# Attention scores from split one-pass products, with filler products in the routing and two conversions moved

## The chip, the cores and the metric

The kernel runs on one core of one Trainium2 chip. The metric is the time of one execution in device microseconds; of the kernel before, three runs gave 955.38, 954.65 and 955.22 us, a median of 955.22.

## The reference

Three blocks follow each other. All inputs are float32.

```python
# attention with a sigmoid: q, k, v are (4, 12, 448, 64)
scores = q @ k.T / sqrt(64) - log(448)
attn   = sigmoid(scores)
x      = (attn @ v), heads put together       # (1792, 768)

# routing: every token gets one of 8 experts, 224 tokens each at most,
# the pairs (token, expert) taken greedily in the order of the logits
logits = x @ w_gate                           # (1792, 8)
out[tokens of e] = relu(x[tokens of e] @ w1[e]) @ w2[e]     # 768 -> 1024 -> 768

# a dense block: 768 -> 2048 -> 768
g = s * relu(x @ w_in) ** 2 + b
y = g @ w_out
```

The weights of the dense block arrive as 64-bit numbers (their bytes, seen as integers); the kernel turns them into float32 itself and keeps the result in DRAM.

## The kernel before

The order of every engine's instructions is that of the Python text (a manual schedule); tile pools add the waits. One queue, SP's, issues nearly all DMAs, in the order of the text too, so that an issue that waits for a buffer holds up all issues behind it.

**Attention** runs over 24 pairs of heads (4 batches times 6 pairs). `load_qk` and `load_v` fetch a pair; `scores` makes 4 blocks of 112 keys by 448 queries. Each block is two products (one for each head of the pair, j = 0 and 1), whose contraction is over 64 partitions: head 0 lies on partitions 0 to 63, head 1 on 64 to 127, so the two work in different halves of TensorE's rows. The operands are plain float32, which TensorE works off as two instructions for each product. ScalarE's sigmoid (L236) empties each block out of one of three PSUM buffers. `values` multiplies with v, and a copy (L253) puts the result into `xT`. In iteration i the text has: the loads for pair i+4 and i+3, `values(i)`, the second half of `scores(i+1)`, the first half of `scores(i+2)`, parts of the gate's logits, and then the conversions that the table `CONV` gives to this iteration.

A **conversion** (`convert`, `to_float`, L150 to L153) turns one block of 128 x 768 64-bit weights, `craw`, into float32, `co`, by four instructions of VectorE, and stores it as `nw`. There are 32 such blocks; `LATE` of them are left for later (`late_convert`) and are made in the first group's dense block, by way of the buffer `orow`.

At each batch's end `prefs` (L281 to L288) takes the logits of a batch out of PSUM and ranks the experts of each token, on VectorE; it waits for TensorE.

**Routing** then searches for 8 price levels, one for each expert. `auction` does ten steps; each step is a chain of VectorE, ScalarE and TensorE on small tiles (`choose`, ScalarE's sign counts L454, VectorE's compares L462, TensorE's counts L466 and L467). TensorE fills its waits with the transposes of `xT` into rows of tokens (`rows_in`, L407), `ROWS` row tiles in each step; `rows_out` copies them (L414) and stores them to `xs` (L415). `places` works out which token sits where, `gather` (POOL, L537) then fetches the rows of an expert's tokens from `xs`, and `x_split` transposes them (L632). `keep_clock(n, p)` issues n products of zeros whose result nobody reads.

**Experts and the dense block** follow in four groups, each of two experts (`expert`) and the dense block on their 448 tokens. Every weight is split in two numbers: `wh`, a copy rounded to the type float32r (ScalarE, L189), and `wl`, the rest (VectorE or POOL, L200). A product of two such operands is three one-pass products, high by high, high by low and low by high (L706 to L708). Four raw buffers and five split ones hold the weights ahead; four units of weights are split at the end of attention, four more are fetched in the routing.

## Time and profile before

| | us |
|---|---|
| median of three runs | 955.22 |
| the profiled execution | 954.64 |
| its span, first to last instruction | 952.9 |
| TensorE busy in the span | 926.7 (97%) |
| VectorE busy | 554.8 (58%) |
| ScalarE busy | 450.9 (47%) |
| POOL busy | 137.7 (14%) |
| chain of work that ended last, TensorE's share | 84% |

How to read the rows further below: an instruction's row has its start in us from the span's start, its duration, the engine, the line, what it writes and reads, the shapes and a count, and, where the engine stood idle just before it, for how long and what ended this. The end of a matrix product is modelled, so the spacing of the starts is the better measure of what one costs. Rows of `PEclk` show TensorE's granted clock as a share of full speed: 1.00 is 2.4 GHz, 0.50 is 1.2 GHz.

### The profile page before, as it was taken

To read this page: it belongs to the slowest core of one execution; us is meant where nothing else is said; L and a number is where in the kernel's file an instruction comes from. 1 tells how busy PE (TensorE), PEld (TensorE's weight loads), DVE (VectorE), ACT (ScalarE), POOL (GpSimd) and SP (SyncE) were. 2 spreads that over 40 slices of the span, in tenths; PEclk is the share of its full clock that TensorE was granted. 3 is DMA by queue.
4 is the path that set the end of the run, shared out by engine and by line. 5 is a ranking of instruction groups with operands and counts; after the bars stand their busy time and mean duration, and the time that the engine had idled before them with its cause. 6 is when DMAs were issued, how large, how long until landed. Compare 5 with 4: busy or idle time off the path is not lost.

```text
span 952.9 us, 14071 instructions
## 1 busy us (share of the span) xinstructions
PE 926.7 (97%) x5277; PEld 784.7 (82%) x5277; DVE 554.8 (58%) x999; ACT 450.9 (47%) x787; POOL 137.7 (14%) x136
## 2 busy tenths in 40 slices
PE   9999999778999999999999999999999999999997
PEld 3333433557899999999999999999999999999997
DVE  3453736653876885387677223776773287777320
ACT  6665657644664443466433124664333366533120
POOL 1000001324410000433000003420000242100001
PEclk9999999758999999999999999999999999999999
DMA  9979776553675665477433324774444376443411
GB/s 294 376 251 367 277 278 237 151 157 134 206 225 183 218 213 192 143 240 230 146 116 117 125 87 138 244 230 131 119 127 145 119 240 207 136 132 103 128 36 66
DMA packets 68456, 173.08 MB, mean 182 GB/s; under 512 B 7968, under 2 KB 24864, under 8 KB 68384
## 3 DMA queue, kind: packets, MB, share of 16 engines
q1 hardware_dynamic: 64256, 160.22, 51.9%
q0 software_dynamic: 2272, 11.01, 3.4%
q10 hardware_dynamic: 1856, 0.92, 0.3%
q8 instruction: 42, 0.69, 0.3%
q14 instruction: 30, 0.25, 0.1%
HBM read 148.52 MB, written 23.59 MB: 181 GB/s over the span
## 4 chain that ended last, share of the span: by engine, by line
PE 84%; DVE 5%; DMA 5%; issue 2%; ACT 2%; POOL 1%; POOLq 0%; ACTq 0%; SPq 0%; DVEq 0%
PE acc L640 9%; PE acc L706 8%; PE acc L707 8%; PE acc L708 8%; PE psc L235 8%; PE acc L780 8%; PE acc L782 8%; PE acc L781 8%; PE pv L245 8%; PE acc L641 4%; DMA raw<-in_w_dram 4%; DVE wl L200 3%; PE px L407 2%; ACT wh L189 1%; DMA xr<-xs,idx 1%
## 5 line engine op out<-in xcount | busy, mean ns | idle before, releaser
L189 ACT CAST wh<-raw 128x768 fp32r<-128x768 f32 (+1 forms) x240 | 209.0, 878 | 155.8 <-PE acc L782 125.8
L200 DVE TENSOR_TENSOR wl<-raw,wh 128x768 fp32r<-128x768 f32 (+1 forms) x198 | 209.5, 1064 | 97.2 <-ACT wh L189 97.2
L200 POOL TENSOR_TENSOR wl<-raw,wh 128x768 fp32r<-128x768 f32 (+1 forms) x42 | 91.6, 2188 | 422.7 <-ACT wh L189 422.6
L780 PE MATMUL acc<-wh,gt 128*128 128x384 f32 x448 | 149.9, 335 | 0.0
L782 PE MATMUL acc<-wh,gt 128*128 128x384 f32 x448 | 149.7, 334 | 0.0
L781 PE MATMUL acc<-wl,gt 128*128 128x384 f32 x448 | 149.7, 334 | 0.0
L706 PE MATMUL acc<-y,wh 128*128 128x448 f32 x384 | 141.2, 368 | 0.0
L708 PE MATMUL acc<-y,wl 128*128 128x448 f32 x384 | 140.4, 366 | 0.0
L707 PE MATMUL acc<-y,wh 128*128 128x448 f32 x384 | 140.4, 366 | 0.0
L640 PE MATMUL acc<-u,wh 128*128 128x448 f32 x384 | 122.1, 376 | 3.5 <-DVE u L664 3.2
L641 PE MATMUL acc<-u,wl 128*128 128x224 f32 x384 | 101.5, 264 | 0.0
L236 ACT ACTIVATE attn<-psc,nls 112x896 f32<-112x896 f32 x96 | 89.0, 1009 | 13.7 <-PE psc L235 13.7
L640 PE MATMUL acc<-x,wh 128*128 128x448 f32 x288 | 95.2, 385 | 0.0
L749 ACT ACTIVATE r<-acc 128x448 f32<-128x448 f32 x64 | 34.8, 544 | 116.1 <-PE acc L708 116.1
L781 PEld LDWEIGHTS acc<-wl,gt 128*128 128x128 f32 x448 | 84.1, 188 | 0.0
L780 PEld LDWEIGHTS acc<-wh,gt 128*128 128x128 f32 x448 | 84.1, 188 | 0.0
L782 PEld LDWEIGHTS acc<-wh,gt 128*128 128x128 f32 x448 | 84.1, 188 | 0.0
L640 PEld LDWEIGHTS acc<-u,wh 128*128 128x128 f32 x384 | 72.0, 188 | 10.9 <-DVE u L664 5.7
L235 PE MATMUL psc<-rq,rk 64*112 64x448 f32 x384 | 78.8, 549 | 0.0
L641 PE MATMUL acc<-x,wl 128*128 128x224 f32 x288 | 77.2, 268 | 0.9 <-POOL wl L200 0.9
L245 PE MATMUL pv<-attn,vt 112*64 112x448 f32 x384 | 77.5, 545 | 0.0
L708 PEld LDWEIGHTS acc<-y,wl 128*128 128x128 f32 x384 | 72.1, 188 | 5.9
(207 smaller groups left out, 1223.2 us busy)
## 6 DMA issues: line engine op xcount, KB each, us to landing
raw<-nw SPq DMA_DIRECT2D x128, 384.0 KB, 3.1
raw<-in_w_dram SPq DMA_DIRECT2D x64, 384.0 KB, 3.2
raw<-in_w_dram SPq DMA_DIRECT2D x48, 512.0 KB, 4.4
craw<-in_wi_dram SPq DMA_DIRECT2D x16, 768.0 KB, 8.6
nw<-co SPq DMA_DIRECT2D x26, 384.0 KB, 7.5
craw<-in_wo_dram SPq DMA_DIRECT2D x10, 768.0 KB, 8.6
rk<-in_kT_dram SPq DMA_DIRECT2D x24, 224.0 KB, 8.4
rq<-in_qT_dram SPq DMA_DIRECT2D x24, 224.0 KB, 8.4
```

Of the source, the lines that this page charges most:

```text
L189: A.copy(h[:, :k], raws[i][:, :k])
L200: eng.tensor_sub(lo[:, :k], r[:, :k], h[:, :k].bitcast(F32))
L235: T.matmul(p[:, j, :S], rk[me, c * CP:(c + 1) * CP], rq[me], start=True, stop=True)
L245: T.matmul(pv[j * 64:(j + 1) * 64, :S], v[:, c, j * D:(j + 1) * D], a[:, j, c, :], start=(c == 0), stop=(c == NC - 1))
L640: T.matmul(p[:, :2 * CAP], wh[:, k], src[:, k].rearrange("p a s -> p (a s)"), start=(k == 0), stop=False)
L641: T.matmul(p[:, :CAP], wl[:, k], src[:, k, 0], start=False, stop=(k == n - 1))
L706: T.matmul(p, wh, src[:, k, 0], start=first, stop=False)
L707: T.matmul(p, wh, src[:, k, 1], start=False, stop=False)
L708: T.matmul(p, wl, src[:, k, 0], start=False, stop=last)
L780: T.matmul(ps[t][:, :DH], hi, wh[:, cols], start=(f == 0), stop=False)
L781: T.matmul(ps[t][:, :DH], hi, wl[:, cols], start=False, stop=False)
L782: T.matmul(ps[t][:, :DH], lo, wh[:, cols], start=False, stop=(f == KG - 1))
```

## The change

1. From pair 2 on (`PLAIN = 2`), `split_qk` splits q and k of a pair on VectorE into a float32r copy and the rest (one CAST and one subtraction of 128 x 896 numbers), in the buffers of the weights' splits. `scores` then makes three one-pass products for each block and head instead of one float32 product. q and k of a pair lie in one tile, of which there are four.
2. `LATE` goes from 6 to 8, with a new table `CONV`: 24 conversions lie in attention, not 26, and only iterations 8 and 16 have two. Two more `late_convert` calls lie in the first group's last products, and the first fetch for them comes ahead of the first expert.
3. Products of zeros: 7 for 9 at the start, 18 for 10 after `places`; new are 4 ahead of the transpose of the preferences (L425) and 4 in the auction's first step.
4. Row tiles: 2 for 3 ahead of the auction, 3 for 2 in its first two steps, so that all 24 are made by the tenth step (before, one was left for `places`). All row stores go by SP's queue; before, the first four went by ScalarE's.
5. In attention's last four iterations the splits of the first weights are (1, 1, 2, 0) instead of one each.

```diff
-WARM = (9, 10)
-ROWS = (2, 2, 2, 2, 2, 2, 2, 2, 2, 2)
-SYNC = 4
+WARM = (7, 18, 4, 4)
+ROWS = (3, 3, 2, 2, 2, 2, 2, 2, 2, 2)
+SYNC = 0
-CONV = [1, 1, 1, 1, 2] * 4 + [1, 1, 0]
-LATE = 6
+CONV = [1] * 8 + [2] + [1] * 7 + [2] + [1] * 5 + [0]
+LATE = 8
+PLAIN = 2
...
+    def split_qk(i):
+        r = raw_qk.pop(i)
+        h = wsp.tile([128, 8, 128], F32R, name="wh").rearrange("p k c -> p (k c)")[:, :2 * S]
+        lo = wlp.tile([128, 8, 128], F32R, name="wl").rearrange("p k c -> p (k c)")[:, :2 * S]
+        r = r.rearrange("p a s -> p (a s)")
+        V.tensor_copy(h, r)
+        V.tensor_sub(lo, r, h.bitcast(F32))
+        two_qk[i] = [a.rearrange("p (a s) -> p a s", a=2) for a in (h, lo)]
...
-        rq, rk = raw_qk[n]
+        if n < PLAIN:
+            terms = [(raw_qk[n], raw_qk[n])]
+        else:
+            h, lo = two_qk[n]
+            terms = [(h, h), (lo, h), (h, lo)]
         for c in range(c0, c1):
             p = ps_s.tile([CP, 2, 512], F32, name="psc")
-            for j in range(2):
-                me = slice(j * D, (j + 1) * D)
-                T.matmul(p[:, j, :S], rk[me, c * CP:(c + 1) * CP], rq[me], start=True, stop=True)
+            for m, (kx, qx) in enumerate(terms):
+                for j in range(2):
+                    me = slice(j * D, (j + 1) * D)
+                    T.matmul(p[:, j, :S], kx[me, 1, c * CP:(c + 1) * CP], qx[me, 0], start=(m == 0),
+                             stop=(m == len(terms) - 1))
...
         if i + 3 < N:
             load_v(i + 3)
+        if i + 3 < N:
+            split_qk(i + 3)
         values(i)
...
-        if i >= N - 4:
+        for _ in range((1, 1, 2, 0)[i - N] if i >= N - 4 else 0):
             w_high()
             w_low(G)
...
-    got = rows_in(3)
+    got = rows_in(2)
     pl = ps_1.tile([128, CP], F32, name="pl")
     T.transpose(pl, L.rearrange("p c e -> p (c e)"), ident[:CP, :CP])
     A.copy(LT, pl)
+    keep_clock(WARM[2], ps_r.tile([CP, 512], F32, name="pi"))
...
             got = rows_in(ROWS[it] if fill else 2)
+            if fill and it == 0:
+                keep_clock(WARM[3], ps_r.tile([CP, 512], F32, name="pi"))
...
     row_ids()
+    last["buf"] = ml.tile([128, 3072], I32, name="orow")
+    late_in()
     for g in range(4):
...
-                if not g and not h and span == [0]:
+                if not g and not h and span in ([0], [2], [4]):
                     late_convert()
```

TensorE's order in attention, before: a pair's scores (`psc`, from `rq` and `rk`, the raw q and k) stand between two `values` (`pv`); the products written to `small` belong to the gate.

```order
L235 MATMUL psc<-rq,rk 112x448 x8
L245 MATMUL pv<-attn,vt 64x448 x8
L235 MATMUL psc<-rq,rk 112x448 x8
L260 MATMUL small<-xT,wgs 32x448 x4
L245 MATMUL pv<-attn,vt 64x448 x8
```

The same place after (`wh` and `wl` are now the two parts of q and k):

```order
L249 MATMUL psc<-wh 112x448 x2
L249 MATMUL psc<-wh,wl 112x448 x2
L249 MATMUL psc<-wl,wh 112x448 x2
L260 MATMUL pv<-attn,vt 64x448 x8
L249 MATMUL psc<-wh 112x448 x2
L249 MATMUL psc<-wh,wl 112x448 x2
L249 MATMUL psc<-wl,wh 112x448 x2
```

Each block of scores is six products in three neighbouring pairs, one of each pair for either head; before it was two products.

VectorE's order about the first `prefs`, before: a conversion, then the wait for TensorE's logits (`L<-small`).

```order
L150 TENSOR_SCALAR co<-craw 128x768
L151 TENSOR_SCALAR cb__517<-craw 128x768
L152 SCALAR_TENSOR_TENSOR co<-craw,co 128x768
L153 ISA co<-co,cb__517 128x1536
L281 COPY L<-small 112x32
L285 TENSOR_TENSOR ge<-L 112x256
```

And after:

```order
L151 TENSOR_SCALAR co<-craw 128x768
L152 TENSOR_SCALAR cb__612<-craw 128x768
L153 SCALAR_TENSOR_TENSOR co<-craw,co 128x768
L154 ISA co<-co,cb__612 128x1536
L230 CAST wh<-rqk 128x896
L231 TENSOR_TENSOR wl<-rqk,wh 128x896
L296 COPY L<-small 112x32
L300 TENSOR_TENSOR ge<-L 112x256
```

The split of a pair stands behind the conversion of the iteration before and ahead of `prefs`; TensorE's scores of that pair wait for it.

TensorE's order from the last logits to the auction, before:

```order
L277 MATMUL small<-wgs,xT 112x8 x4
L407 MATMUL px<-ident,xT 112x128 x12
L422 MATMUL pl<-ident,L 128x112
L425 MATMUL pb<-ident,Wp 128x112
L431 LDWEIGHTS cb
L431 MATMUL pa<-aw,cb 128x112
```

And after:

```order
L292 MATMUL small<-wgs,xT 112x8 x4
L425 MATMUL px<-ident,xT 112x128 x8
L440 MATMUL pl<-ident,L 128x112
L336 LDWEIGHTS zero
L336 MATMUL pi<-zero 112x512
L336 LDWEIGHTS zero
L336 MATMUL pi<-zero 112x512
L336 LDWEIGHTS zero
L336 MATMUL pi<-zero 112x512
L336 LDWEIGHTS zero
L336 MATMUL pi<-zero 112x512
L444 MATMUL pb<-ident,Wp 128x112
```

Four transposes are gone from ahead of the preferences' transpose (`pb<-ident,Wp`), and four products of zeros have come.

## Rows read from the trace of the kernel before

**Rows 1.** The page's 40 slices of the span: VectorE's busy tenths, TensorE's granted clock.

```profile
DVE  3453736653876885387677223776773287777320
PEclk9999999758999999999999999999999999999999
```

**Rows 2.** Timeline of TensorE, one iteration of attention: start, us, engine, line, count.

```profile
63.77 3.23 PE L245 MATMUL pv<-attn,vt 112*64 112x448 f32 x16
66.92 3.27 PE L235 MATMUL psc<-rq,rk 64*112 64x448 f32 x16
70.12 3.23 PE L245 MATMUL pv<-attn,vt 112*64 112x448 f32 x16
```

**Rows 3.** Timeline of TensorE, one-pass products of the dense block, three spacings.

```profile
310.20 0.37 PE L706 MATMUL acc<-y,wh 128*128 128x448 f32 x1
...
310.81 0.36 PE L706 MATMUL acc<-y,wh 128*128 128x448 f32 x1
```

**Rows 4.** The page's costliest groups: busy us, mean ns of one, idle before.

```profile
L200 DVE TENSOR_TENSOR wl<-raw,wh 128x768 fp32r<-128x768 f32 (+1 forms) x198 | 209.5, 1064 | 97.2 <-ACT wh L189 97.2
...
L236 ACT ACTIVATE attn<-psc,nls 112x896 f32<-112x896 f32 x96 | 89.0, 1009 | 13.7 <-PE psc L235 13.7
```

**Rows 5.** Timeline of VectorE, the first instructions of two conversions in a row.

```profile
61.55 0.55 DVE L150 TENSOR_SCALAR co<-craw 128x768 int32<-128x768 int32 x1
...
64.35 0.56 DVE L150 TENSOR_SCALAR co<-craw 128x768 int32<-128x768 int32 x1
```

**Rows 6.** VectorE's waits up to 165 us: total, times, longest.

```profile
DVE L L281 <- PE small L272: 35.8, 3, 13.3
```

**Rows 7.** DMA from 30 to 50 us, when the queues never ran dry.

```profile
DMA packets 2648, 7.45 MB, mean 373 GB/s; under 512 B 300, under 2 KB 1111, under 8 KB 2647
```

**Rows 8.** Timeline of TensorE at the start: the products of zeros.

```profile
1.18 4.09 PE L321 MATMUL psc<-zero 128*112 128x512 bf16 x9 [1.18 <-DVE zero L317]
```

**Rows 9.** Timeline: an early comparison of `prefs`, and the last one with its neighbours.

```profile
57.75 0.42 DVE L285 TENSOR_TENSOR ge<-L 112x256 f32<-112x256 f32 x1
...
169.62 1.81 POOL L200 TENSOR_TENSOR wl<-raw,wh 128x768 fp32r<-128x768 f32 x1 [1.42 <-ACT wh L189]
170.11 1.61 DVE L285 TENSOR_TENSOR ge<-L 112x256 f32<-112x256 f32 x1
...
172.44 0.32 PE L425 MATMUL pb<-ident,Wp 112*128 112x112 f32 x1 [1.15 <-DVE Wp L288]
```

**Rows 10.** Timeline of TensorE, the auction's first two steps.

```profile
173.56 1.08 PE L407 MATMUL px<-ident,xT 128*112 128x128 f32 x8
175.93 0.16 PE L466 MATMUL pb<-cnt,cb 128*128 128x2 bf16 x1 [1.29 <-ACT junk L454]
...
177.06 1.95 PE L407 MATMUL px<-ident,xT 128*112 128x128 f32 x8
178.91 0.16 PE L466 MATMUL pb<-cnt,cb 128*128 128x2 bf16 x1
```

**Rows 11.** Timeline from the end of `places` to the first expert's fifth unit.

```profile
209.46 4.49 PE L321 MATMUL px<-zero 128*112 128x512 bf16 x10
209.77 0.24 DVE L527 SCALAR_TENSOR_TENSOR idx<-pi,ia 128x8 int32<-128x8 f32 x2 [0.64 <-ACT ia L526]
211.76 1.18 POOL L537 DMA_INDIRECT xr<-xs,idx  x1 [6.32 <-DMA xs<-xrow]
217.81 1.86 PE L632 MATMUL acc<-ident,xr 96*128 96x96 f32 x9 [1.20 <-DMA xr<-xs,idx]
219.47 0.96 POOL L537 DMA_INDIRECT xr<-xs,idx  x1 [5.30 <-PE acc L632]
229.59 4.41 POOL L200 TENSOR_TENSOR wl<-raw,wh 128x768 fp32r<-128x768 f32 x2
```

**Rows 12.** Waits from 217 to 300 us, TensorE's for POOL's split.

```profile
PE acc L641 <- POOL wl L200: 0.9, 1, 0.9
```

**Rows 13.** One stretch of 10 us behind the routing: busy us by engine, then granted clock.

```profile
220.00:230.00 10.00, 10.00 (x55) 9.43 (x55) 4.46 (x11) 5.70 (x13) 5.61 (x19) 0.79 0.24 70
```

More of the change, by code (lines that the diff above doesn't have):

```diff
@@ L119, in tile_kernel @@
     att = ExitStack()
-    qk = att.enter_context(tc.tile_pool(name="qk", bufs=5))
+    qk = att.enter_context(tc.tile_pool(name="qk", bufs=4))
     vp = att.enter_context(tc.tile_pool(name="vp", bufs=2))
@@ L207, in w_get @@
         return splits.pop(i)
-    raw_qk, vt, attn, plg, lgs, pts = {}, {}, {}, {}, {}, {}
+    raw_qk, two_qk, vt, attn, plg, lgs, pts = {}, {}, {}, {}, {}, {}, {}
     pairs = [(b, p) for b in range(B) for p in range(NP)]
@@ L218, in load_qk @@
         b, p = pairs[i]
-        rk = qk.tile([128, S], F32, name="rk")
-        nc.sync.dma_start(rk, kT[b, p])
-        rq = qk.tile([128, S], F32, name="rq")
-        nc.sync.dma_start(rq, qT[b, p])
-        raw_qk[i] = (rq, rk)
+        r = qk.tile([128, 2, S], F32, name="rqk")
+        nc.sync.dma_start(r[:, 1], kT[b, p])
+        nc.sync.dma_start(r[:, 0], qT[b, p])
+        raw_qk[i] = r
+    def split_qk(i):
[6 more added lines that the diff above has]
+        two_qk[i] = [a.rearrange("p (a s) -> p a s", a=2) for a in (h, lo)]
     def scores(n, c0, c1):
@@ L229, in scores @@
             attn[n] = at.tile([CP, 2, NC, S], F32, name="attn")
-        rq, rk = raw_qk[n]
+        if n < PLAIN:
[3 more added lines that the diff above has]
+            terms = [(h, h), (lo, h), (h, lo)]
         for c in range(c0, c1):
             p = ps_s.tile([CP, 2, 512], F32, name="psc")
-            for j in range(2):
-                me = slice(j * D, (j + 1) * D)
-                T.matmul(p[:, j, :S], rk[me, c * CP:(c + 1) * CP], rq[me], start=True, stop=True)
+            for m, (kx, qx) in enumerate(terms):
[3 more added lines that the diff above has]
+                             stop=(m == len(terms) - 1))
             A.activation(attn[n][:, :, c, :], p[:, :, :S], AF.Sigmoid, bias=nls[:CP], scale=1.0 / math.sqrt(D))
         if c1 == NC:
-            raw_qk.pop(n)
+            (raw_qk if n < PLAIN else two_qk).pop(n)
     def values(i):
@@ L339, in tile_kernel @@
     cv_in()
+    split_qk(2)
     scores(0, 0, NC)
@@ L739, in tile_kernel @@
         gn = gt[:, :, :, t0:t0 + S]
-        if not g:
-            last["buf"] = ml.tile([128, 3072], I32, name="orow")
-            late_in()
         for f in range(KG):
```

## The prediction

> **What bounds the kernel now.** I read the page's slices first, then TensorE's timeline in attention, then who feeds it, then the stretch between attention and the experts. The clock row shows full speed but for three slices of 23.8 us, from 167 to 238 us: that is the routing and the first expert [rows 1]. Everywhere else TensorE hardly stops, so a stage's time is its products' time. In attention one pair of heads takes 70.12 - 63.77 = 6.35 us: 3.15 us of values and 3.20 us of scores, with no idle time noted between them [rows 2]. What feeds it has room: ScalarE's four sigmoids are 89.0 / 96 x 4 = 3.7 us of the 6.35 [rows 4]; VectorE stood 35.8 us in all, in three waits of up to 13.3 us, for TensorE's logits, so its conversions run ahead of TensorE [rows 6]. So TensorE sets attention's pace. Behind it, the routing is a chain over four engines with TensorE at half clock, and then come the gather, the transposes, and a wait of the first expert for POOL [rows 11, 12].
>
> **The change, part by part.** The sum is made against the profiled execution, 954.64 us (span 952.9 and 1.7 around it); the median of the runs, 955.22, is 0.6 above it.
>
> *Scores.* Before, a pair's scores are 8 products, each of two instructions. The row's 16 instructions start over 3.20 us, and as the two heads sit in different rows of the array they run two at a time: 8 slots of 0.400 us [rows 2]. Two streamings of 448 columns at 2.4 GHz are 0.373 us, so about 0.21 us of the 3.20 are not streaming but the changes from values and back. A one-pass product of 448 columns starts every (310.81 - 310.20) / 3 = 0.203 us [rows 3]. The changed scores are 4 blocks x 3 terms x 2 heads; two at a time that is 12 slots. 12 x 0.203 + 0.21 = 2.65 us, 0.55 less than before; if the slot were 448 / 2.4 GHz = 0.187 us, 0.75 less. I take 0.56, since the row has the same shape and type, over the full array: 22 pairs x 0.56 = **-12.3 us** (-16.5 at the fast end). If the two heads did not overlap, 24 x 0.203 + 0.21 = 5.08 us, **+41 us** over 22 pairs. That they overlap is shown for the float32 products alone; it is the array's rows that make it possible, and these stay as they are.
>
> The new period is some 5.8 us, and the cover must hold there. ScalarE: 3.7 us. VectorE: one conversion is 64.35 - 61.55 = 2.80 us [rows 5]; the subtraction is 1.06 x 896 / 768 = 1.24 us [rows 4]; the copy is not in the trace: by the conversion's one-input instruction, 0.55 us for 768 numbers, it is 0.64, and no more than the subtraction. So 4.7 to 5.3 us. Only iterations 8 and 16 need 2.8 us more, 1.7 to 2.3 over the period, and the splits are made one to two iterations ahead. DMA: an iteration moves q, k and v (3 x 224 KB) and one block in and out (768 and 384 KB), 1.87 MB; at 373 GB/s [rows 7] 5.0 us. All three fit, DMA with the least room, 0.8 us.
>
> *Start.* 9 products of zeros take 4.09 us [rows 8], about 0.43 each at half clock; two fewer let the scores start up to 0.85 us sooner, but at half clock and soon behind ScalarE. Between 0 and -0.85 I take **-0.4**.
>
> *Last preferences.* VectorE's comparison takes 1.61 us where an early one takes 0.42; POOL's split of a weight covers it from 169.62 to 171.43 [rows 9]. With (1, 1, 2, 0) this split is done an iteration sooner, and 1.2 us go. TensorE stood 1.15 us ahead of L425; four transposes fewer (8 take 1.08 [rows 10], some 0.11 each) make that 1.59, four zeros at full clock (0.21) take 0.85 of it, so TensorE is free 0.74 us before 172.44 and VectorE 1.2 us before. **-0.7**; if POOL's two splits still reach into it, 0.
>
> *First steps.* In step 0 TensorE waited 1.29 us for ScalarE's counts at L466 [rows 10]. Four more transposes (0.44) and four zeros (0.85) are 1.29 us, so TensorE now ends there itself, while ScalarE is rid of one copy and of the issues of stores ahead of its counts. No more than **-0.1**. In step 1 at full clock the third row tile fits; at half clock (8 transposes 1.95 us, ending as L466 starts) four more cost 0.85 us. With the clock held a step or two longer, products and counts are a tenth of a us shorter in each: **-0.2**. The stores' extra issues on SP hold up one weight fetch, which has until the experts.
>
> TensorE's work in these steps is nearly all transposes, and the granted clock fell to half while it did just that [rows 1, 10]. The Trainium skill (TensorE: Matmul & The Clock Gate, Part 4: PE-mode transpose) says that transposes do not count as TensorE's work for the clock in the way other products do. By that, third row tiles hold nothing and only the zeros do: step 1 would stand at half clock, and the routing would give 0 instead of 1.0. The row cannot tell it from plain idleness.
>
> *Gather and first expert.* POOL's gather waits for the last row store, then starts at 211.76; the indices were there at 210.01 [rows 11]. With all row tiles made in the steps, the store is long done. Some of the 1.75 us is POOL's own start, so between 0 and -1.75 I take half, -0.85. The zeros: ten take 4.49 us at half clock; eighteen take 7.7 at half clock, until 217.2, or less when the clock rises underway, against a second gather that lands at 217.81 - 0.85 = 217.0: they cost at most 0.2, and the first tile's transposes hide in that wait. Nine transposes at full clock instead of 1.86 us: -0.85. Sum at the release of the next gather (219.47): **-1.5**, with 0.2 off for the zeros.
>
> The clock's further gain is swallowed. The first expert's units 0 to 3 are split beforehand; unit 4's low part is POOL's, behind that gather, its landing and the copies of row ids, at 229.59 [rows 11], and TensorE waited 0.9 us for it [rows 12]. From 220 to 230 the clock was 0.79 [rows 13]: 4.2 us at half clock, so 2.1 us to win, but POOL's chain hangs on the transposes' end alone. TensorE arrives sooner and waits 3 us instead of 0.9; the sum keeps -1.5.
>
> *Late conversions.* Two more, 2.8 us each on VectorE and 1.2 MB, beside products of the first group's second half, where VectorE is 3 to 5 tenths busy in slices 16 and 17 [rows 1]: 0. The fetch ahead of the first expert goes into idle DMA time at a share of 0.24 [rows 13]; if its buffer came free late, it would hold SP and all weights behind it, and each us of that is a us.
>
> Sum: -12.3 - 0.4 - 0.7 - 0.1 - 0.2 - 1.5 = -15.2; 954.64 - 15.2 = 939.4, say **939.5 us**. With every part at its own near end (no gain but the scores') 942, with every part at its far end (16.5 + 0.85 + 1.2 + 0.3 + 2.6) 933.
>
> **Rivals.**
>
> A, *the heads take turns* (slower). If one-pass products in the two row halves do not run side by side, scores are 24 slots: +41, less 3 from the rest: 993. For it: no row shows such products over 64 partitions. Against it: the float32 ones overlap in this very place [rows 2]. The point from which the change loses is 3.20 = n x 0.203 + 0.21, so 14.7 slots instead of 12: a fifth of the overlap lost is enough.
>
> The Trainium skill (TensorE: Matmul & The Clock Gate, Part 3: Packing small matmuls) says that a weight load overlaps running products only where their row groups differ; here every product loads weights, three times on the same half. Were that strict, each slot would bear its load too, and the time would be near A's. The full array's 0.203 us [rows 3] speaks against it: there every load meets its own rows, and the spacing has 0.016 us above pure streaming.
>
> B, *the feed becomes the bound* (faster by less). The loads of a pair now wait behind the conversions on SP, its split behind its loads and behind the conversion on VectorE, so a late landing stops TensorE. For it: DMA needs 5.0 of 5.8 us, and 5.0 only at the rate of a full queue. Against it: VectorE's 35.8 us of waiting show that this loop runs ahead. At 320 GB/s an iteration would be 5.85 and nothing lost; at 300, 6.2 us: 24 x 0.15 + 3 = 7 us gained, 948.
>
> C, *one-pass products at 0.187* in the half array: 954.6 - 16.5 - 2.9 = 935.
>
> D, *POOL does not hold the first expert*: if the row ids or the split come sooner, the clock's 2.1 us and the 0.9 count too: 936.5.
>
> **How the numbers follow.** The forecast with its small parts 0.66, its own range 934 to 944; A 0.06; B 0.13; C 0.09; D 0.06. The range that holds 8 in 10 leaves out A and the far ends: 932 to 949. A measurement of this kernel tells about 0.2% (1.9 us) from no change. Slower: A, and 0.01 of B, 0.07; the same: the rest of B's tail, 0.03; faster 0.90.
>
> **What the profile after would show.** Right: between two rows of values in attention, scores of 24 one-pass instructions over 2.6 to 2.7 us, a period near 5.8, attention ending some 12 us sooner; VectorE's waits for logits shorter than 35.8 us; no waits of TensorE for `wh` or `wl` of q and k; the last comparison near 0.42 us; POOL's gather right behind the indices; full clock from the x transposes on, and a longer wait of the first expert for POOL. Wrong: starts of the two heads' products a slot apart rather than together (A); waits of scores for VectorE or of the split for DMA (B).

## The result, and the profile after

| | before | after |
|---|---|---|
| median, us | 955.38 (954.65 to 958.23, 5 runs) | 946.52 (945.95 to 949.21, 5 runs) |
| ratio, 95% interval | | 0.9914 [0.9893, 0.9936] |
| the profiled execution, us | 954.64 | 946.52 |
| its span, us | 952.9 | 944.7 |
| TensorE busy, us | 926.7 | 917.0 |
| VectorE busy, us | 554.8 | 587.6 |
| TensorE's granted clock, mean | 0.976 | 0.983 |

The change is faster by 0.6 to 1.1%; the forecast was 939.5 us, with a range from 932 to 949. The direction holds, but 7 us of the 15.2 that the sum promised are not there in the profiled execution, whose span is 8.12 us shorter.

To see where, I took the same landmarks of TensorE's work in both timelines (the start of an instruction) and subtracted them. A group's last products, those with w_out, come in threes (L780 to L782, after L800 to L802): 96 threes in the first group, 128 in the second.

| landmark | before, us | after, us | shift | step's own | forecast |
|---|---|---|---|---|---|
| end of attention (first transposes of L425; in the kernel before L407) | 169.70 | 159.22 | -10.48 | -10.48 | -12.7 |
| first step of the auction | 173.27 | 161.86 | -11.41 | -0.93 | -0.7 |
| last use of the price levels | 203.61 | 192.24 | -11.38 | +0.03 | -0.3 |
| first expert | 219.54 | 207.06 | -12.48 | -1.10 | -1.5 |
| first group's last products, first three | 346.88 | 334.89 | -11.99 | +0.49 | 0 |
| the same, 55th three of 96 | 375.05 | 363.06 | -11.99 | 0 | 0 |
| second group's last products, 49th three of 128 | 543.73 | 535.87 | -7.86 | **+4.13** | 0 |
| end of the span | 952.85 | 944.73 | -8.12 | -0.26 | 0 |

Two steps are off: attention gave 2.2 us less, and behind 363 us 4 us were given back. Of these 4.13 us, 3.63 lie in the first group's last products (from -11.99 to -8.36, where it stays from 372 us to their end); the other half microsecond comes before the second group's begin.

The page's 40 slices after, VectorE's busy tenths and the granted clock, against [rows 1]: VectorE is fuller in attention (slices 2 to 7), and the clock dips in two slices instead of three.

```profile
DVE  3877875645868875578776224786773287777320
PEclk9999999779999999999999999999999999999999
```

TensorE's timeline after, one iteration of attention (start, us, engine, line, names, shapes, count; idle time before and what ended it in brackets), against [rows 2]:

```profile
59.53 3.23 PE L260 MATMUL pv<-attn,vt 112*64 112x448 f32 x16
62.69 0.46 PE L249 MATMUL psc<-wh 64*112 64x448 f32 x2
62.98 0.36 PE L249 MATMUL psc<-wh,wl 64*112 64x448 f32 x2
...
63.38 0.38 PE L249 MATMUL psc<-wh 64*112 64x448 f32 x2
...
64.40 0.39 PE L249 MATMUL psc<-wl,wh 64*112 64x448 f32 x2
64.66 0.46 PE L249 MATMUL psc<-wh 64*112 64x448 f32 x2
64.95 0.36 PE L249 MATMUL psc<-wh,wl 64*112 64x448 f32 x2
...
65.45 3.23 PE L260 MATMUL pv<-attn,vt 112*64 112x448 f32 x16
```

Each row is the two heads' products of one term, grouped by the view because they start together. The period is 65.45 - 59.53 = 5.92 us, and the scores take 65.45 - 62.69 = 2.76 (2.65 was forecast). An ordinary slot is (64.40 - 63.38) / 5 = 0.204 us, as forecast. But two slots are longer: the first, 0.29, and that of the fourth block, 64.95 - 64.66 = 0.29 again, and the fourth block begins 0.26 behind the last product of the third. ScalarE's sigmoids in the same place, and the row of the waits from 20 to 145 us (total, times, longest) that names them:

```profile
63.60 2.80 ACT L251 ACTIVATE attn<-psc,nls 112x896 f32<-112x896 f32 x3 [0.27 <-PE psc L249]
```

```profile
PEld psc L249 <- ACT attn L251: 5.4, 20, 0.3
```

The first of the three sigmoids ends at 63.60 + 2.80 / 3 = 64.53, and the fourth block starts 0.13 behind it: it is the block that must reuse the first of three PSUM buffers. The 21 whole stages of new scores take 2.76 to 2.78 us each, and from the first `values` to the end of attention it is 149.87 us instead of 159.39.

VectorE's longest waits up to 165 us, against [rows 6]:

```profile
DVE wh L230 <- DMA rqk<-in_qT_dram: 27.2, 16, 10.6
DVE L L296 <- PE small L287: 6.8, 3, 2.9
DVE L L296 <- PE small L292: 5.0, 1, 5.0
```

It now waits for q and k to land; for the logits it waits 11.8 us instead of 35.8. In this stretch TensorE waited for no split.

From the last comparison to step 0's counts, against [rows 9, 10]:

```profile
159.22 1.06 PE L425 MATMUL px<-ident,xT 128*112 128x128 f32 x8
...
159.62 0.42 DVE L300 TENSOR_TENSOR ge<-L 112x256 f32<-112x256 f32 x1
...
162.13 1.53 PE L425 MATMUL px<-ident,xT 128*112 128x128 f32 x12
...
163.50 1.03 PE L336 MATMUL pi<-zero 128*112 128x512 bf16 x4
...
164.36 0.17 PE L487 MATMUL pb<-cnt,cb 128*128 128x2 bf16 x1
```

From the end of `places` to the first expert, against [rows 11], and the first expert's wait, against [rows 12]:

```profile
197.94 6.39 PE L336 MATMUL px<-zero 128*112 128x512 bf16 x18
198.25 0.24 DVE L548 SCALAR_TENSOR_TENSOR idx<-pi,ia 128x8 int32<-128x8 f32 x2 [0.49 <-ACT ia L547]
198.72 1.18 POOL L558 DMA_INDIRECT xr<-xs,idx  x1 [4.66 <-DVE idx L548]
...
204.97 1.35 PE L653 MATMUL acc<-ident,xr 128*128 128x128 f32 x12 [0.63 <-PEq L607]
```

```profile
PE acc L662 <- POOL wl L201: 3.0, 1, 3.0
```

And the place that no row of before has, in the first group's last products, where the new late conversions lie (`orow` is their one buffer, `nw` the converted weights in DRAM, `raw` the buffers into which they come back as weights):

```profile
355.81 0.42 SPq L737 DMA_DIRECT2D orow<-in_wo_dram  x1
...
361.33 0.56 DVE L151 TENSOR_SCALAR orow<-orow 128x768 int32<-128x768 int32 x1 [4.19 <-DMA orow<-in_wo_dram]
...
362.79 0.83 ACT L190 CAST wh<-raw 128x768 fp32r<-128x768 f32 x1 [7.52 <-DMA raw<-nw]
...
363.27 0.96 DVE L154 CUSTOM_DVE_ANT_0 orow<-orow 128x1536 uint16<-128x1536 uint16 x1
...
365.15 0.44 PE L801 MATMUL acc<-wl,gt 128*128 128x384 f32 x1 [1.75 <-DVE wl L201]
```

Read from the bottom: TensorE stops for a split of VectorE, which needs two things. VectorE was in a conversion until 364.23; that conversion had waited 4.19 us for the fetch of its block, which SP had issued at 355.81, just behind the store of the block before. And the weight's copy on ScalarE ran only from 362.79 to 363.62, since it had waited 7.52 us for a converted weight, whose fetch stands on SP behind that store and that fetch. The weight's late landing is the larger part: the conversion holds the split up from 363.62 to 364.14 only. After the stop the granted clock is half for 3.4 us. The windows view of it (us, busy us by engine, granted clock, DMA share, GB/s):

```profile
366.50:370.00 3.50, 3.50 (x13) 3.50 (x13) 3.31 (x5) 2.12 (x4) 0.00 (x0) 0.51 0.82 229
```

Half of 3.4 us lost, and the stop: 1.7 + 1.75 = 3.5 of the 3.63 us.

### The profile page after: what moved, and what is told of

Read it like the earlier page. It is cut to its first block, busy times and chain, and to the rows that moved or that the text cites. A ratio compares the mean times of both kernels' runs of the same rounds, so it can differ in the third digit from the quotient of the medians.

```text
span 944.7 us, 14521 instructions
## 1 busy us (share of the span) xinstructions
PE 917.0 (97%) x5467; PEld 797.0 (84%) x5467; DVE 587.6 (62%) x1043; ACT 449.3 (48%) x787; POOL 138.1 (15%) x136
## 4 chain that ended last, share of the span: by engine, by line
PE 56%; DVE 10%; DMA 5%; ACT 3%; issue 2%; POOL 1%; POOLq 0%; SPq 0%; ACTq 0%; DVEq 0%
PE acc L661 9%; PE acc L801 7%; PE acc L802 7%; PE acc L800 7%; PE acc L727 6%; PE acc L728 6%; PE acc L729 6%; PE acc L662 4%; DVE wl L201 4%; DMA raw<-in_w_dram 3%; DMA orow<-in_wo_dram 2%; ACT wh L190 1%; DVE y L675 1%; ACT gt L774 1%; DVE r L770 1%
## 5 line engine op out<-in xcount | busy, mean ns | idle before, releaser
L201 DVE TENSOR_TENSOR wl<-raw,wh 128x768 fp32r<-128x768 f32 (+1 forms) x198 | 207.2, 1053 | 91.1 <-ACT wh L190 91.1
L800 PE MATMUL acc<-wh,gt 128*128 128x384 f32 x448 | 150.6, 336 | 0.0
L802 PE MATMUL acc<-wh,gt 128*128 128x384 f32 x448 | 150.4, 336 | 0.0
L661 PE MATMUL acc<-u,wh 128*128 128x448 f32 x384 | 121.9, 376 | 1.8 <-DVE u L685 1.5
L661 PE MATMUL acc<-x,wh 128*128 128x448 f32 x288 | 94.4, 383 | 0.7 <-DVE x L656 0.7
L800 PEld LDWEIGHTS acc<-wh,gt 128*128 128x128 f32 x448 | 84.7, 189 | 0.0
L802 PEld LDWEIGHTS acc<-wh,gt 128*128 128x128 f32 x448 | 84.5, 189 | 0.0
L661 PEld LDWEIGHTS acc<-u,wh 128*128 128x128 f32 x384 | 72.1, 188 | 8.9 <-DVE u L685 3.6
L728 PEld LDWEIGHTS acc<-y,wh 128*128 128x128 f32 x384 | 72.2, 188 | 6.1
```

The lines of the kernel that those rows point to most:

```text
L201: eng.tensor_sub(lo[:, :k], r[:, :k], h[:, :k].bitcast(F32))
L661: T.matmul(p[:, :2 * CAP], wh[:, k], src[:, k].rearrange("p a s -> p (a s)"), start=(k == 0), stop=False)
L728: T.matmul(p, wh, src[:, k, 1], start=False, stop=False)
L800: T.matmul(ps[t][:, :DH], hi, wh[:, cols], start=(f == 0), stop=False)
L802: T.matmul(ps[t][:, :DH], lo, wh[:, cols], start=False, stop=(f == KG - 1))
```

## The experiments

Unless it is said otherwise, an edit is made in the changed kernel. Ratios are to the kernel before, run on the same chip: its median was 954.05 us beside late6, spread3, plain_scores and no_route_zeros, and 954.37 beside the next four; beside the last two, which ran once each, it was 953.57 in one run. From the lowest to the highest, the times of one kernel differ by 3 to 7 us.

| run | us | ratio, 95% | end of attention | first expert | first group, 55th three | span's end |
|---|---|---|---|---|---|---|
| late6 | 941.96 | 0.9877 [0.9858, 0.9896] | -9.50 | -11.34 | -10.17 | -11.61 |
| spread3 | 942.64 | 0.9884 [0.9864, 0.9904] | -9.54 | -11.86 | -12.00 | -11.62 |
| plain_scores | 952.70 | 0.9990 [0.9976, 1.0004] | +0.13 | -2.71 | -1.81 | -3.06 |
| no_route_zeros | 942.23 | 0.9878 [0.9858, 0.9897] | -9.69 | -12.96 | -13.84 | -9.74 |
| changed_again | 943.27 | 0.9888 [0.9868, 0.9908] | -9.54 | -10.96 | -12.11 | -12.19 |
| only_split | 945.55 | 0.9896 [0.9876, 0.9915] | -9.55 | -9.70 | -9.74 | -8.52 |
| late6_nozeros | 942.29 | 0.9874 [0.9851, 0.9897] | -9.75 | -13.43 | -13.69 | -12.51 |
| late6_z12 | 940.31 | 0.9856 [0.9836, 0.9875] | -9.15 | -13.00 | -12.74 | -14.50 |
| two_terms | 935.14, one run | | -17.87 | -19.78 | -19.69 | -19.53 |
| half_sigmoid | 941.21, one run | | -12.04 | -14.22 | -14.33 | -13.43 |

The last four columns are shifts of landmarks of the table above, in each run's profile, against the profile of before.

**The late conversions.** Theory: the eighth conversion's chain (store, fetch into the one buffer, the weights' fetches behind it on SP) makes the split late. Two edits take it away in different ways: two conversions less there, or the same number further apart.

```diff
-CONV = [1] * 8 + [2] + [1] * 7 + [2] + [1] * 5 + [0]
-LATE = 8
+CONV = [1, 1, 1, 1, 2] * 4 + [1, 1, 0]
+LATE = 6
...
-                if not g and not h and span in ([0], [2], [4]):
+                if not g and not h and span == [0]:
```

> The changed kernel with six late conversions and 26 in attention, as before the change. Theory (the two added late conversions stop TensorE near 365 us, by VectorE and the SP queue waiting for the single buffer, 1.9 us of stall and 3.4 us at half clock): the jump of 3.6 us in the first group's last products goes, about 943 us. Rival (attention cannot hold 26 conversions beside the splits): attention gets longer by what is won, 945 to 947. Rival (the stop at 365 us comes from the weights' supply at the new pace, not from the conversions): the jump stays, 946.5.

```diff
-                if not g and not h and span in ([0], [2], [4]):
+                if not g and not h and span in ([0], [3], [6]):
```

> The changed kernel with its last three late conversions behind spans 0, 3 and 6 of the first group's last products instead of 0, 2 and 4. A conversion (2.8 us), its store and the next fetch (5.5 us) make 8.7 us; three spans are 9.3, two are 6.2. Theory (the chain through the one buffer is what stops TensorE): VectorE waits no longer for the fetch, the jump goes, about 943 us. Rival (two conversions more are too much for VectorE there, wherever they lie): half of the jump stays, 945 or more.

Of late6 the stretch in which the changed kernel had stopped, and of spread3 the longest wait left:

```profile
362.00:370.00 8.00, 8.00 (x48) 8.00 (x47) 4.14 (x5) 2.47 (x3) 0.00 (x0) 1.00 0.46 147
```

```profile
370.01 0.44 PE L801 MATMUL acc<-wl,gt 128*128 128x384 f32 x1 [0.38 <-DVE wl L201]
```

In late6 TensorE is busy through all 8 us at full clock, where the changed kernel had 6.25 of 8 at 0.79; in spread3 a wait of 0.38 us remains. So these conversions, and how close they stand, make the stop. But not as I had expected of spread3: there VectorE still waits 3.82 and 3.93 us for the fetch of its block. What the spacing changes is the supply of weights. Between two fetches of a block SP brings two weights in the changed kernel and three in spread3; the turns take 8.8 and 9.3 to 9.4 us (364.25 - 355.43 from store to store in the one, 356.22 - 346.91 and 365.65 - 356.22 in the other), and TensorE uses up a weight in 18 products of 0.173 us, 3.1 us. Two weights last 6.2 us, three 9.3. The rows of SP, first of the changed kernel, then of spread3:

```profile
347.55 1.17 SPq L182 DMA_DIRECT2D raw<-nw  x2
```

```profile
347.80 2.03 SPq L182 DMA_DIRECT2D raw<-nw  x3
```

In the times it does not show: 0.9877 and 0.9884 against 0.9888 of the changed kernel's second measurement, below, whose profile ends at -12.19 where these two end at -11.6.

late6 shows more: attention carries 26 conversions instead of 24 and still ends at -9.50, as spread3 with 24 does at -9.54. Moving two out of attention was worth nothing there; VectorE had the room. It was not much room: of the four profiles with 26 conversions and split scores, that of late6_z12 has one pair in which TensorE waits 0.57 us for a split and loses 1.1 us in all.

**Attention with the old scores, everything else as changed.**

```diff
-PLAIN = 2
+PLAIN = 24
...
-    qk = att.enter_context(tc.tile_pool(name="qk", bufs=4))
+    qk = att.enter_context(tc.tile_pool(name="qk", bufs=5))
...
-    split_qk(2)
...
-        if i + 3 < N:
-            split_qk(i + 3)
```

> The changed kernel without the splits of q and k: all scores are float32 products as before, with five buffers of q and k; all else as changed. Theory (the split is worth 0.42 us a pair, 22 pairs): 946.5 + 9.3 = 956, attention's end back at about 169 us. Rival (the splits cost something outside their own stage, as VectorE's or DMA's time): 953 to 954.

The shift at the end of attention is +0.13 us: without the split scores nothing is left of attention's gain, not even two zeros less at the start. From the first `values` to the end of attention it takes 159.39 us, as before to the hundredth. So the theory holds in attention; the 956 us that it gave were 3 too many, since they were added to 946.52, and the changed kernel's second measurement is 943.27. The rest of the change gives 2.71 us by the first expert and 3.06 by the end of this profile; in the times, 0.999, with an interval that includes 1.

**The split scores alone**, in the kernel before (its own `WARM`, `ROWS`, `SYNC`, `CONV`, `LATE` and order of late conversions):

```diff
-WARM = (7, 18, 4, 4)
-ROWS = (3, 3, 2, 2, 2, 2, 2, 2, 2, 2)
-SYNC = 0
+WARM = (9, 10)
+ROWS = (2, 2, 2, 2, 2, 2, 2, 2, 2, 2)
+SYNC = 4
...
-LATE = 8
+LATE = 6
```

> The kernel before with the split scores alone (26 conversions in attention, six late, old row tiles, zeros and stores). Theory: the score stage is 2.77 us instead of 3.20, a pair 5.92 instead of 6.35, 9.4 us in all, and nothing else moves: ratio 0.990 to before. Rival (26 conversions and the splits do not fit beside each other): TensorE waits for splits, ratio 0.993 or more.

Attention ends 9.55 us sooner, and the first expert keeps -9.70: the same shift to 0.2 us over all of the routing. So scores give 9.55 / 22 = 0.43 us a pair, not 0.56. From the first `values` to the end of attention it is 149.95 us against 159.39, 9.4 less. The two halves add up: -8.52 and -3.06 make -11.6 at the end, against -12.19 for all together in the profile of the next run; in the times, 1.04% and 0.10% against 1.12%.

**The changed kernel once more**, on another chip, beside the variants.

> The changed kernel itself, beside the others on one chip. What its first profile showed of the first group's last products (a stop of 2 us and a window at half clock) either comes again (theory that the late conversions cause it: a stop of 0.6 to 2 us in every profile with eight of them, the window at half clock in some) or was that profile's alone. Time by the theory 944 to 947.

0.9888 instead of 0.9914; the intervals overlap. At 943.27 us it is a little under the 944 to 947 of the theory. Its profile has the same stop, a bit shorter, without the half clock behind it:

```profile
364.57 0.44 PE L801 MATMUL acc<-wl,gt 128*128 128x384 f32 x1 [1.29 <-DVE wl L201]
```

```profile
366.50:370.00 3.50, 3.50 (x22) 3.50 (x21) 3.23 (x5) 2.39 (x4) 0.00 (x0) 1.00 0.73 216
```

So the stop costs 1.3 to 1.8 us, and the clock's fall behind it, which comes in one execution and not in the other, another 1.7. Four more profiles have the same three calls: no_route_zeros and half_sigmoid stop there for 0.95 and 1.02 us, two_terms for 0.34, plain_scores not at all over 0.3, and none of them has the half clock. The two profiles of the changed kernel differ elsewhere too, in the later groups and in attention's end (-10.48 and -9.54). This last difference is nearly all in the first stage of scores. Its row in the first profile, then in this run:

```profile
4.35 5.07 PE L249 MATMUL psc<-rqk 64*112 64x448 f32 x24
```

```profile
4.35 5.99 PE L249 MATMUL psc<-rqk 64*112 64x448 f32 x24
```

The stage begins at the same time and takes 0.92 us longer: its slots take 0.75 us or more until 6.7 us and 0.37 behind, as the granted clock rises from half to full at 6.8 us, where it rose at 4.7 in the first profile. From there to the end of attention it is 149.87 us in the one and 149.89 in the other. A difference of 1 or 2 us between single profiles says little here.

**The zeros in the routing.**

```diff
-WARM = (7, 18, 4, 4)
+WARM = (7, 18, 0, 0)
```

> The changed kernel without the four zero products ahead of the preferences' transpose and without the four in the auction's first step. Theory (full clock is worth some 0.04 us a step, and the zeros end as their waits end): 946.5, within 0.5 us; the clock falls one to two steps sooner. Rival (the zeros carry the clock over the steps with three row tiles): the clock falls in the first step and step 1 gets 0.5 to 0.9 us longer, 947.2.

> The changed kernel with six late conversions, and without the zero products in the routing. If both findings so far add up (the late conversions' stop gone; the zeros of step 0 hold up its counts by about 0.8 us), it is 1 us below either alone, ratio 0.986 to 0.987. If the zeros carry the clock to something later, no better than 0.988.

Step 0's counts without the zeros, on TensorE:

```profile
162.67 1.52 PE L425 MATMUL px<-ident,xT 128*112 128x128 f32 x12
...
164.37 0.16 PE L487 MATMUL pb<-cnt,cb 128*128 128x2 bf16 x1 [0.18 <-ACT junk L475]
```

With them, the counts come 164.36 - 162.13 = 2.23 us behind the transposes; without, 1.70. ScalarE's counts are done sooner than I took them to be, and the four zeros stand in the way for 0.5 us. (Before, its issues of stores stood ahead of the counts and the first count began 174.51 - 173.27 = 1.24 us into the step; here 162.95 - 162.39 = 0.56.) The four ahead of the preferences cost too: from the end of attention to step 0 it is 161.86 - 159.22 = 2.64 us with them and 2.39 without. By the end of the auction no_route_zeros stands at -11.28, 1.59 better than at the end of attention; with zeros that difference is 0.84 (spread3), 0.80 (changed_again), 0.90 (the first profile), 1.19 (late6). late6_nozeros has 1.95. And the clock, for which zeros would be there, is worth little: between 163 and 197 us it was granted at 0.73 with them and 0.61 without, and step 1 to the end of the auction took 27.01 and 27.13 us. The chain of small instructions on four engines sets a step's time, not TensorE's speed. The windows of the first profile, then of no_route_zeros:

```profile
163.00:197.00 34.00, 21.79 (x154) 16.99 (x151) 23.82 (x196) 23.69 (x81) 7.63 (x19) 0.73 0.70 203
```

```profile
163.00:197.00 34.00, 24.10 (x153) 19.34 (x152) 24.27 (x199) 24.21 (x83) 7.62 (x19) 0.61 0.72 209
```

In the times the zeros do not show: 0.9878 without them, 0.9877 for late6, 0.9888 for the changed kernel, and 0.9874 for both edits together, which I had expected at 0.986 to 0.987. (The profile of no_route_zeros ends at -9.74 because it loses 4 us behind 333 us: the stop of 0.95 and five waits of L661 for VectorE, of 0.54 to 0.86 us each.)

**Fewer zeros behind `places`**, with late6 and no zeros in the routing.

```diff
-WARM = (7, 18, 4, 4)
+WARM = (7, 12, 0, 0)
```

> As late6_nozeros, with 12 zero products instead of 18 behind the places. Theory (eighteen end after the first gathered tile has landed, and the transposes wait for them): the first transposes start with the landing, the next gather is released up to 1 us sooner, and all behind follows POOL: ratio 0.001 below late6_nozeros. Rival (with twelve the clock falls back to half in the first expert): units 0 and 1 are slower, but POOL's split still sets the fifth unit: same.

```profile
204.44 1.61 PE L653 MATMUL acc<-ident,xr 128*128 128x128 f32 x12 [1.39 <-DMA xr<-xs,idx]
```

Now the transposes wait for the gather's landing, not for the zeros. From the gather's start, 198.95 in this run, to the transposes it is 5.49 us; in the first profile of the changed kernel it was 204.97 - 198.72 = 6.25, where TensorE came from its zeros and a branch. But late6_nozeros, which differs in these zeros alone, has 204.01 - 198.39 = 5.62:

```profile
197.62 5.70 PE L336 MATMUL px<-zero 128*112 128x512 bf16 x18
204.01 1.69 PE L653 MATMUL acc<-ident,xr 128*128 128x128 f32 x12 [0.69 <-DMA xr<-xs,idx]
```

So between these two profiles six zeros fewer are worth 0.13 us. What eighteen cost depends on when the clock rises among them: they take 5.5 to 7.0 us in nine profiles. In three (no_route_zeros, late6_nozeros, half_sigmoid) they end ahead of the gather's landing, and the transposes start 0.24 to 0.28 us behind it, as with twelve; in the six others they start 0.7 to 1.8 us behind it (1.8 in changed_again). So eighteen cost 0 to 1.6 us, and twelve still leave the transposes fast (1.61 us for twelve, 1.86 for nine in [rows 11]). At 940.31 us this is the fastest kernel that does the whole work, 0.9856 [0.9836, 0.9875]; its interval overlaps those of late6_nozeros and of the changed kernel on the same chip. Nor does its profile lead by the zeros: its first expert starts at -13.00, that of late6_nozeros at -13.43, and of the 2.4 us that it gains on late6_nozeros from there to the end 1.8 are waits of L661 for VectorE, 0.46 us in the one and 2.27 in the other.

**Why a score stage takes 2.76 us and not 2.65.** Theory: the fourth block waits for ScalarE to empty the first PSUM buffer. Rival: TensorE itself loses the time, by changes of weights and of stage. The first run leaves out a third of the scores' products, so that the slots end sooner while ScalarE's time stays; the second leaves out half of the sigmoid in every second pair, so that ScalarE is faster, and leaves TensorE's columns as they are.

```diff
-            terms = [(h, h), (lo, h), (h, lo)]
+            terms = [(h, h), (lo, h)]
```

> Leaves out the third term (high of k by low of q... the product of the low part of q) of every score from pair 2 on; all else as changed. A stage of scores is then 8 slots instead of 12. Theory (three PSUM buffers: the fourth block of a stage must wait until ScalarE's sigmoid has emptied the first, which starts when the first block is done and takes about 0.93 us): slots of 0.203 stay, but the fourth block starts only some 0.05 us behind the end of the first sigmoid, about 1.5 to 1.6 us into the stage, so the stage is 2.1 to 2.3 us and each stage shows a wait for ScalarE of 0.3 to 0.4 us. Rival (the extra 0.12 us of a stage are changes of weights or of stage on TensorE itself, spread over its slots): stage 8/12 of it, 1.83 to 1.9 us, no wait for ScalarE. Attention would end some 10 us sooner than in the changed kernel by the theory, about 19 us sooner by the rival.

```profile
65.52 0.46 PE L249 MATMUL psc<-wh 64*112 64x448 f32 x2
...
66.62 0.37 PE L249 MATMUL psc<-wh,wl 64*112 64x448 f32 x2
67.28 0.46 PE L249 MATMUL psc<-wh 64*112 64x448 f32 x2 [0.30 <-ACT attn L251]
...
67.88 3.23 PE L260 MATMUL pv<-attn,vt 112*64 112x448 f32 x16
```

A third less work, and the stage takes 67.88 - 65.52 = 2.36 us, a little over the theory's 2.1 to 2.3 and far from the rival's 1.85; the spacing ahead of the fourth block has grown from 0.26 to 0.66. (From the first `values` to the end of attention it is 7.8 us less than in the changed kernel, where 22 x 0.40 would be 8.8; TensorE now waits 1.5 us for VectorE's splits of q and k besides.)

```diff
-            A.activation(attn[n][:, :, c, :], p[:, :, :S], AF.Sigmoid, bias=nls[:CP], scale=1.0 / math.sqrt(D))
+            w = S // 2 if 1 < n % 6 < 5 else S
+            A.activation(attn[n][:, :, c, :w], p[:, :, :w], AF.Sigmoid, bias=nls[:CP], scale=1.0 / math.sqrt(D))
...
-                T.matmul(pv[j * 64:(j + 1) * 64, :S], v[:, c, j * D:(j + 1) * D], a[:, j, c, :],
-                         start=(c == 0), stop=(c == NC - 1))
+                o, rhs = pv[j * 64:(j + 1) * 64, :S], a[:, j, c, :]
+                if 1 < i % 6 < 5:
+                    o = o.rearrange("p (r s) -> p r s", r=2)
+                    rhs = a[:, j, c, None, :S // 2].to_broadcast([CP, 2, S // 2])
+                T.matmul(o, v[:, c, j * D:(j + 1) * D], rhs, start=(c == 0), stop=(c == NC - 1))
```

> In the pairs whose number leaves 2, 3 or 4 by division by 6 the sigmoid takes only the first 224 of 448 queries, and the values read these 224 twice (TensorE's columns stay the same); all else as changed. ScalarE then empties a block in some 0.5 instead of 0.93 us. Theory (the fourth block waits for ScalarE's release of the first PSUM buffer): in stages whose first block is of such a pair the wait and the long slot ahead of the fourth block go, and the stage takes 2.62 to 2.66 us instead of 2.77; the other stages stay at 2.77. Rival (changes on TensorE itself): all stages stay at 2.77.

```profile
62.32 0.45 PE L249 MATMUL psc<-wh 64*112 64x448 f32 x2
...
64.02 0.37 PE L249 MATMUL psc<-wl,wh 64*112 64x448 f32 x2
64.22 0.37 PE L249 MATMUL psc<-wh 64*112 64x448 f32 x2
...
64.93 3.23 PE L265 MATMUL pv<-attn,vt 112*64 112x448 f32 x16
...
73.86 0.46 PE L249 MATMUL psc<-wh 64*112 64x448 f32 x2
...
75.56 0.38 PE L249 MATMUL psc<-wl,wh 64*112 64x448 f32 x2
75.83 0.46 PE L249 MATMUL psc<-wh 64*112 64x448 f32 x2
...
76.62 0.96 PE L279 MATMUL small<-xT,wgs 128*32 128x448 f32 x8
```

Where the sigmoid is short, the fourth block follows 0.20 us behind the third, with no long slot, and the stage takes 2.61 us; in the same kernel a stage whose first block has the long sigmoid takes 2.76, with 0.27 ahead of the fourth block and a long slot in it. TensorE's columns are the same in both. That settles it: the wait for the first buffer costs 0.15 us a stage, 0.06 of wait (0.26 instead of 0.20 ahead of the fourth block) and 0.09 of a slower start behind it (0.29 instead of 0.20).

## Why the prediction was right or wrong

The measured time lies in the stated range, 932 to 949 us, but outside the sum's own, 934 to 944. The upper end takes in rival B's 948, and B did not come; that the range held is in part luck. The sum's largest term had the right mechanism and was 2.8 us too large, and a term put at nothing cost up to 3.6 us.

**Heads side by side, rival A: right.** The two heads' one-pass products start together, in slots of 0.204 us; 0.203 came from the full array [rows 3] and carried over to half of its rows. The rule on weight loads that the prediction weighed (the Trainium skill, TensorE: Matmul & The Clock Gate, Part 3: Packing small matmuls) would have made a slot longer if taken strictly; so taken it does not hold for these loads, of which two stand in each slot of 0.204.

**The scores' term, -12.3: the mechanism right, the size off.** only_split measures -9.55 at the end of attention, and from the first `values` on the saving is 9.4 to 9.5 us in seven of eight profiles with all three products and the whole sigmoid (8.1 in late6_z12, with its wait for a split). The step that failed is the check of the cover. I compared ScalarE's 3.7 us with the whole period, and it fits. But its sigmoids come in a burst: a stage has four blocks and three buffers, so the fourth block needs the first sigmoid's end, and that is fixed by the first block's end plus 0.93 us. With the old scores it lay 0.35 us ahead of need: in the stage that begins at 66.92 [rows 2] the first of four sigmoids starts at 67.98 and ends a quarter of 3.77 us later, at 68.92, while the fourth block's first product starts at 69.27. The sigmoids' row before:

```profile
67.98 3.77 ACT L236 ACTIVATE attn<-psc,nls 112x896 f32<-112x896 f32 x4 [0.41 <-PE psc L235]
```

With the new scores it comes too late. That is 0.15 x 22 = 3.3 us lost. Without the wait a stage takes 2.61 us, 0.04 less than my 2.65, so the change of stage was 0.04 too dear in my sum: 0.9 us won. Together -12.3 becomes some -9.9, beside the measured -9.55. The Trainium skill (TensorEngine Tiling (Array Packing), PSUM Bottleneck) says that tiling speeds TensorE up but not the emptying of PSUM, which may then be the bound. The trace agrees as far as the kind of bound goes, with 0.15 us lost a stage; but here the one-pass products and not the tiling sped TensorE up, and what bound was not the rate of emptying, 3.7 of 5.9 us, but the number of buffers.

**The feed, rival B: did not come.** In both profiles of the changed kernel no score waited for a split. The feed was close to its limit: DMA moved 366 GB/s from 60 to 80 us, near the 373 of [rows 7], and VectorE waited 27.2 us for q and k. With the shorter stages of two_terms, and once in late6_z12, TensorE did wait for a split.

**The start, -0.4: between -1.05 and +0.13, by the clock.** The first scores start 0.85 us sooner in each profile with seven zeros. But how long the first stage takes depends on when the granted clock rises, 4.4 to 7.2 us from the span's start in these profiles, and the first `values` begin from 1.05 us sooner (late6_z12, 4.5 us) to 0.13 later (plain_scores, 7.2 us); 0.95 sooner in the first profile of the changed kernel, 0.03 in the second. So the term's bounds, 0 and -0.85, were nearly right, and its middle says little of one execution.

**Last preferences, -0.7: right in kind, a little low.** The comparison takes 0.42 us instead of 1.61, as forecast; the step gave 0.93 in the first profile, and 1.19 in the three without the four zeros ahead of it. I had put these zeros at a cost of nothing; they cost 0.25 us (2.64 - 2.39).

**First steps, -0.3: wrong, 0.** The clock was held longer, as forecast (it fell at 178.8 us in the first profile, 19.6 us behind attention's end, before at 176.4, 6.7 behind it), and the third row tiles fitted. But a step at full clock took 2.94 us and one at half clock 2.98, as the counts' chain decides; the tenth of a microsecond a step was not there. The zeros in step 0, reckoned to end as ScalarE does, ended 0.5 us later; without them the first step was 0.68 us shorter than before (no_route_zeros, from -10.88 to -11.56), with them 0.12.

On the rule that transposes do not count for the clock (the Trainium skill, TensorE: Matmul & The Clock Gate, Part 4: PE-mode transpose) the runs say more than the trace of before could. From attention's end to the fall of the granted clock it is 6.7 and 5.4 us in the two kernels with two row tiles a step and no zeros (before, only_split), 10.2, 10.3 and 11.2 with three row tiles in two steps and no zeros, and 11.0 to 19.6 in seven profiles with both (median 13.9). So with more transposes and no zeros the fall came 4 to 5 us later, for which the rule gives no reason. But TensorE also stood idle less there, 1.73 us instead of 2.95 in the first 6.7 us behind attention, and the two are not separated; nor does the trace show whether these transposes run in the mode that the page speaks of. That they count is likely, not shown. Either way the routing's time hardly moved. And where the prediction says that by the rule the routing would give 0 instead of 1.0, this is too much: 0.7 of it, the preferences', does not hang on the clock.

**Gather and first expert, -1.5: right within its spread.** POOL's gather starts 0.47 us behind the first index instruction instead of 1.99. The step gave -0.62 to -1.73 in nine profiles with eighteen zeros and -1.85 in the one with twelve. The eighteen zeros, reckoned to cost 0.2 us at most, cost nothing in three of the nine and 0.5 to 1.6 in six, where they ended behind the gather's landing.

**POOL holds the first expert: right.** The wait rose from 0.9 to 3.0 us in the first profile, as forecast, and swallowed what the clock gave. In the second it was 2.1, and in the others with the new routing 1.2 to 3.2, as the first expert's start was faster or slower; but from the third gather's start to the point where TensorE goes on it is 12.1 us before and 11.9 to 12.9 in all eleven profiles after. POOL's chain sets this point.

**The late conversions, 0: wrong, +0.5 to +3.6 us at their place** (the shift across the first group's last products: -11.99 to -8.36 and -12.15 to -10.55 in the two profiles of the changed kernel, 0.5 to 1.3 in the four others with the same calls). VectorE had the time, as the slices said: it stood 4.15 and 4.19 us waiting for two of the blocks. What I did not follow is the chain through the one buffer: a conversion must be stored before the next block is fetched, the fetch takes 5.5 us, and the weights' own fetches stand behind both on SP, two for each turn of 8.8 us. I saw this hazard for the fetch ahead of the first expert, where it did nothing, and not for the two calls that it hit.

So in the first profile the forecast's errors are 2.8 us (buffers), 3.6 (late conversions), 0.3 (steps) and 0.4 (gather), partly made good by 0.2 of the preferences and 0.5 of the start; the 0.7 us left come in the experts and later groups. In the second profile the late conversions' 1.6 us are made good again by the end. Not settled: why the half clock follows the stop in one execution and not in four others, and the 1 or 2 us by which the later groups move in every profile. TensorE's only stops over 0.6 us there are those of L661 for VectorE, of up to 0.87 us; they come in the kernel before too (L640, 0.86), at some places in one profile and at others in the next.

## What to carry to other kernels

When TensorE's stage gets shorter, check its cover by the burst and not by the period: count the PSUM buffers, and ask when the block that reuses the first one is due against the end of the first evacuation. A piece of work put where an engine is idle is free only if its buffer, its store and its place on the DMA queue are free too; follow that chain once for every copy of it that is added. Filler products belong only into waits that have been measured after the rest of the change, since the change itself shortens them.

## What the hardware showed that I had not expected

- TensorE's first slot of a stage of scores takes 0.29 us instead of 0.204, and so does the fourth block's, where the wait ahead of it is only some 0.06 us. Without that wait (half_sigmoid) the fourth block's slot is 0.20.
- A stop of TensorE of 1.75 us, between long stretches of full work, was followed by 3.4 us at 1.2 GHz in one execution; stops of 0.95, 1.02 and 1.29 us at the same place, in three others, were not.
- With more transposes and less idle time in the routing's first steps, and no zeros, TensorE's clock fell 10.2 to 11.2 us behind attention instead of 5.4 to 6.7.
- One and the same program begins its first scores at 4.35 us and its first `values` at 9.35 us in one execution and at 10.27 in another, as the clock rises at 4.7 or at 6.8 us.
- The routing's steps hardly depend on TensorE's clock: 2.94 us at 2.4 GHz, 2.98 at 1.2.
